# Inverse transform tables by two DMA transposes, smaller first loads, an earlier centroid chain, a last tile stored in halves and a new instruction order

## The chip, the cores and the metric

The kernel runs on one core of a Trainium2 chip. The metric is the device time of one execution in microseconds (us), the median over several runs. The engines are named PE (TensorE, the matrix engine), PEld (its loading of weights, which overlaps matmuls), DVE (VectorE), ACT (ScalarE), POOL (GpSimd) and SP (SyncE, which here only issues transfers). ACT, POOL and SP each have a queue of DMA transfers that they issue.

## The reference, cut to what matters

Clustered attention for 4 batches, 8 heads, 768 rows and 64 columns, then a gated long convolution (a "Hyena" block) over the 768 rows of the 512 joined columns.

```python
# attention: q, k, v [4, 8, 768, 64], centroids [8, 16, 64]
q_n, k_n, c_n = ...                       # each divided by its norm + 1e-6
q_assign = argmax(einsum('bhsd,hcd->bhsc', q_n, c_n), -1)
k_assign = argmax(einsum('bhsd,hcd->bhsc', k_n, c_n), -1)
mask = q_assign[:, :, :, None] == k_assign[:, :, None, :]
attn = softmax(where(mask, q @ k.T / 8, -1e9))
x = (attn @ v) -> [4, 768, 512]
# gate: w_proj [512, 1536], filter_fft [768, 512], w_out [512, 512]
x1, x2, x3 = split(x @ w_proj, 3)
conv = irfft(rfft(x2, 768) * rfft(filter_fft, 768), 768)
out = (x1 * conv * x3) @ w_out            # [4, 768, 512]
```

## The kernel before

**Stages.** The 32 heads of the four batches are taken as eight groups n of four heads, each with two pairs pr of heads, so there are 16 attention passes. A pass goes over six tiles sk of 128 keys. For each key tile PE makes three score products of 128x512 (L689), ACT takes the exponential of each (L698, L701) into one of five buffers p, PE multiplies p with v (L712, four matmuls into one pair of banks), and DVE adds p to a running sum acc (L729 for the first two tiles, L733 after), from which the softmax denominators come (L746 in some passes). The mask is part of the score product: the operands aug hold q or k with extra rows that carry the one-hot cluster of each row (L615 to L658; the one-hot codes are transposed by a DMA, L658).

**Routing.** Before a group's scores, q and k are loaded (load_qk, L299), transposed on PE (L584, L595), multiplied with the normalized centroids in the block table cbd (L504), and the similarities are transposed back (L514) and turned into one-hot codes by DVE (L521 and after). The first group's masks go another way, through first_masks (L494).

**The gate.** After every second group one batch is complete, and hyena (L820) does its gate: forward transform U (L846), products with the spectrum of the filter (L876 into tm, L880 into y), the inverse transform I (L930 to L936), its folding (L942, L952), the gate product y2 (L955), the output product W (L967), a copy to ob (L975) and the store to HBM (L978, L982). Three gates run as filler between attention passes of the next groups; the last has nothing beside it.

**Transform tables.** No FFT is done: the forward table fw and the inverse table inv hold cosines and sines of the 768-point transform, split into even and odd parts. In angles (L345), DVE reduces the angles and ACT takes sines into fw. In tables (L383), six PE operations of 16 transposes in all (L402, L405) turn fw into inv, and eight copies by ACT or DVE (L409, L413) bring the pieces from the banks. tables also loads the filter and makes its spectrum (spectrum, L472).

**Start.** Four loads of 196 KB bring q and k of the first two heads, two each, one head at a time, spread over the idle queues of SP and ACT. centroids (L315) loads the 128x64 centroids on ACT's queue and makes cbd: squares, a sum, a square root on ACT, a Newton step on DVE, a transpose on PE (L336) and two copies on DVE (L339, L340). Those DVE operations stand in one queue with the angle operations of angles.

**Order.** The program records each operation with the engines that may do it, its modelled duration and a due time (Plan.op, L85). place (L114) then lays them out greedily, one engine queue at a time, by due time and modelled readiness. NUDGE shifts the due time of single operations by their number, and ONLY fixes the engine of single operations. So an operation that is added or removed, or a change in a modelled cost, can move any other, and which of ACT, DVE and POOL does an eviction is open except where ONLY fixes it. Each engine does its queue in that order. PE's array works as one 128x128 tile or as two 64-column tiles (product, L70); the placing models a small cost for a change between them.

**End.** With `last` set, the inverse of the last gate sums in the banks (L932), so its fold needs no sd. The last pair of output tiles is stored tile by tile (256 KB each, L978), the others two tiles at once (512 KB, L982).

Of the kernel before, what the change touches and what calls it, by code (L numbers as in the profile page):

```python
# [16 lines left out]
BF16 = mybir.dt.bfloat16  # L17
# [15 lines left out]
NV = 3  # L33
# [3 lines left out]
FIRST = 2  # L37
BUSY = 0.0
# [3 lines left out]
ONLY = {23:"SP",24:"SP",25:"SP",30:"SP",55:"ACT",56:"POOL",59:"ACT",62:"POOL",63:"DVE",75:"ACT",76:"ACT",81:"ACT",83:"DVE",84:"DVE",85:"DVE",87:"ACT",89:"DVE",123:"ACT",125:"DVE",131:"DVE",132:"DVE",134:"DVE",143:"ACT",145:"ACT",149:"ACT",151:"ACT",157:"ACT",161:"ACT",163:"ACT",178:"DVE",179:"DVE",228:"ACT",229:"DVE",235:"POOL",240:"POOL",241:"ACT",246:"POOL",247:"ACT",249:"ACT",250:"DVE",292:"DVE",357:"DVE",358:"POOL",359:"DVE",394:"DVE",404:"ACT",405:"ACT",407:"DVE",409:"DVE",410:"POOL",412:"DVE",416:"ACT",417:"ACT",420:"ACT",462:"POOL",464:"DVE",509:"ACT",514:"ACT",523:"DVE",525:"DVE",526:"DVE",533:"POOL",541:"POOL",549:"DVE",556:"ACT",560:"ACT",563:"DVE",567:"ACT",575:"ACT",578:"POOL",579:"POOL",580:"DVE",582:"ACT",595:"DVE",597:"ACT",601:"ACT",605:"ACT",609:"DVE",610:"DVE",612:"ACT",619:"ACT",624:"ACT",640:"DVE",641:"DVE",690:"ACT",691:"ACT",692:"POOL",693:"ACT",694:"POOL",695:"POOL",697:"DVE",699:"DVE",700:"ACT",701:"ACT",703:"POOL",705:"DVE",747:"DVE",810:"DVE",859:"ACT",860:"ACT",861:"ACT",863:"POOL",864:"ACT",866:"ACT",868:"ACT",871:"DVE",872:"ACT",874:"ACT",916:"POOL",917:"DVE",918:"DVE",965:"DVE",975:"ACT",989:"DVE",990:"POOL",997:"DVE",998:"POOL",1006:"DVE",1008:"ACT",1019:"POOL",1020:"POOL",1021:"DVE",1023:"ACT",1027:"ACT",1035:"DVE",1036:"POOL",1042:"ACT",1046:"ACT",1049:"DVE",1051:"DVE",1053:"DVE",1057:"ACT",1061:"ACT",1064:"DVE",1070:"DVE",1075:"ACT",1078:"ACT",1096:"DVE",1098:"DVE",1146:"ACT",1147:"ACT",1148:"POOL",1150:"ACT",1153:"ACT",1154:"DVE",1156:"ACT",1158:"POOL",1159:"DVE",1162:"ACT",1203:"DVE",1204:"DVE",1205:"DVE",1265:"POOL",1266:"POOL",1314:"ACT",1317:"POOL",1319:"ACT",1322:"ACT",1323:"ACT",1324:"ACT",1326:"POOL",1327:"ACT",1328:"POOL",1330:"ACT",1331:"ACT",1372:"DVE",1373:"DVE",1374:"DVE",1431:"ACT",1435:"DVE",1438:"DVE",1445:"POOL",1446:"POOL",1454:"POOL",1462:"DVE",1464:"ACT",1468:"ACT",1472:"ACT",1475:"POOL",1476:"DVE",1477:"DVE",1483:"ACT",1490:"POOL",1491:"DVE",1492:"DVE",1494:"ACT",1505:"DVE",1506:"DVE",1507:"DVE",1509:"ACT",1517:"ACT",1521:"DVE",1526:"ACT",1529:"ACT",1531:"ACT",1534:"ACT",1536:"ACT",1553:"DVE",1554:"POOL",1601:"ACT",1602:"ACT",1603:"ACT",1604:"ACT",1605:"POOL",1606:"DVE",1607:"ACT",1611:"ACT",1612:"POOL",1613:"ACT",1617:"ACT",1652:"POOL",1713:"DVE",1715:"DVE",1772:"POOL",1809:"ACT",1825:"ACT",1831:"ACT",1837:"DVE",1838:"DVE",1845:"POOL",1853:"POOL",1854:"POOL",1862:"DVE",1869:"ACT",1873:"DVE",1878:"ACT",1886:"ACT",1891:"ACT",1899:"ACT",1904:"ACT",1921:"ACT",1925:"ACT",1932:"ACT"}  # L42
THIRDS = [[(0, 0, 512)], [(0, 512, 768), (1, 0, 256)], [(1, 256, 768)]]
HOLD = {"score": "score", "o": "o"}
AFTER = {"PE": .16}
OVERLAP = {"ACT": .09, "DVE": .08}
MODES = {"pv": 64, "bc": 64, "half": 64, "sim": 32, "den": 32, "score": 0, "proj": 0, "inv": 0}


def array(o, last):  # L50

    return MODES.get(o.kind, 128) or (last if last in (64, 128) else 64)

class Op:
    __slots__ = ("eng", "fn", "due", "deps", "outs", "left", "ready", "end", "start", "on",
                 "alloc", "free", "lat", "lock", "byts", "seq", "kind", "whole", "soft")
# [18 lines left out]
class Plan:  # L78
# [6 lines left out]
    def op(self, eng, fn, due, r=(), w=(), alloc=None, free=(), lock=False, byts=0, after=(), kind=None, lat=0.0):  # L85
# [7 lines left out]
        o.lat = lat  # L93
# [20 lines left out]
    def place(self, free0, banks_for, switch=0.1, wait=0.1, rate=215e3, bonus=0.0, margin=0.02195, shape=0.0):  # L114
        free = dict(free0)
        bank_free = [0.0] * 8
        ready = {e: [] for e in free}
        pend = 0
        st = SimpleNamespace(pool=0.0, dve=0.0, bw={}, last=None, kind=None, score=0, o=0, tail=0,
                             held=dict(score=0, fill=0, o=0))  # L120
# [57 lines left out]
        while any(ready.values()):  # L178
            best = None
            for e, lst in ready.items():  # L180
                f = free[e]
                cand = []
                for o in lst:
                    t = max(f, o.ready)
# [24 lines left out]
            take(o)  # L209
            d = o.eng[e]  # L210
            if e == "PE":
                mode = array(o, st.last)
# [1016 lines left out]
```

## Time and profile before

| | |
|---|---|
| time, median of 3 runs | 382.1 us (381.96 to 382.62) |
| the profiled execution, its span | 380.2 us |
| instructions | 8604 |
| PE, PEld | 363.1 us (96%), 208.0 us (55%) |
| DVE, ACT, POOL | 342.1 us (90%), 267.3 us (70%), 104.8 us (28%) |
| DMA | 47.19 MB, mean 124 GB/s |
| costliest on PE: PV product (L712), scores (L75) | 142.3 us, 73.8 us |
| costliest on DVE: running sums (L733) | 112.5 us, 64 of 1758 ns |
| costliest on ACT: exponentials (L701, L698) | 108.3 us, 57.3 us |

The busy time of an engine is the union of its instructions' times in one profiled execution. The time on the first row is taken without a profile, so the two are close but not the same quantity. Lines of a view of the timeline read: start in us, busy us, engine, line of the code, operation, output, inputs, shapes, number of instructions in the row and, in brackets, the idle time ahead of it and what ended that. Lines of a table by stretches read: from and to in us, length, then busy time and count of PE, PEld, DVE, ACT and POOL, the granted clock of PE as a share of full speed, the mean busy share of the DMA engines, and GB/s. A row on one line of the code reads: least/median/greatest duration in ns, and the first and last start in us.

### The profile page before, as it was taken

How to read it: one execution, taken by the hardware profiler on the slowest of the kernel's cores; microseconds unless marked ns; L12 is line 12 of the kernel's file. 1: busy time of each engine (PE TensorE's matmuls, PEld its weight loads, DVE VectorE, ACT ScalarE, POOL GpSimd, SP SyncE). 2: the span in 40 equal slices, each digit the busy share in tenths (PEclk: the TensorE clock that was granted, in tenths of full speed). 3: DMA queues.
4: the chain of work that ended last, by engine and by line, in shares of the span. 5: the costliest groups of instructions: out<-in, count | busy, mean ns of one | idle time of the engine just before them, and what ended most of it. 6: DMA issues, size and time to landing. Idle time of an engine off the chain costs nothing.

```text
span 380.2 us, 8604 instructions
## 1 busy us (share of the span) xinstructions
PE 363.1 (96%) x3303; PEld 208.0 (55%) x3308; DVE 342.1 (90%) x510; ACT 267.3 (70%) x497; POOL 104.8 (28%) x147
## 2 busy tenths in 40 slices
PE   2799999999999999999999999999999999999995
PEld 2464356445445565655565565565465556566682
DVE  8797997987899999989999999998999998899992
ACT  4896989887886778888757569788864667523332
POOL 8410202122031352231311442333210532202600
PEclk9999999999999999999999999999999999999999
DMA  8527973943869666766776967836646741110314
GB/s 218 124 81 174 207 165 90 189 129 62 208 128 156 117 117 141 125 132 108 167 130 118 239 162 136 166 69 91 104 58 172 123 117 15 46 43 2 127 42 166
DMA packets 93861, 47.19 MB, mean 124 GB/s; under 512 B 82088, under 2 KB 87676, under 8 KB 93820
## 3 DMA queue, kind: packets, MB, share of 16 engines
q1 hardware_dynamic: 88620, 37.03, 40.6%
q0 software_dynamic: 2704, 8.98, 16.7%
q10 hardware_dynamic: 2496, 0.62, 0.7%
q8 instruction: 26, 0.43, 0.5%
q14 instruction: 15, 0.12, 0.1%
HBM read 31.59 MB, written 7.40 MB: 103 GB/s over the span
## 4 chain that ended last, share of the span: by engine, by line
PE 84%; DVE 8%; ACT 4%; issue 1%; DMA 1%; ACTq 0%; POOL 0%; DVEq 0%; POOLq 0%
PE pair L712 32%; PE bank L75 32%; PE bank L584 4%; PE bank L846 4%; PE bank L73 3%; PE bank L615 3%; ACT p L701 2%; PE bank L628 1%; PE bank L595 1%; ACT p L698 1%; PE bank L746 1%; DMA rb<-dr 1%; DVE tm L876 1%; PE bank L504 1%; ACT aug L266 1%
## 5 line engine op out<-in xcount | busy, mean ns | idle before, releaser
L712 PE MATMUL pair<-p,vraw 128*64 128x385 f32 x768 | 142.3, 490 | 0.8 <-ACT osb L736 0.5
L701 ACT ACTIVATE p<-bank 128x512 f32<-128x512 f32 x192 | 108.3, 609 | 26.5 <-PE bank L75 21.8
L733 DVE TENSOR_TENSOR acc<-p,acc 128x1536 f32<-128x1536 f32 x64 | 112.5, 1758 | 6.2 <-ACT p L701 1.6
L712 PEld LDWEIGHTS pair<-p,vraw 128*64 128x64 f32 x768 | 53.6, 136 | 49.0 <-issue 40.9
L75 PE MATMUL bank<-aug,aug 80*64 80x256 bf16 (+3 forms) x680 | 73.8, 327 | 0.6 <-ACT p L701 0.5
L698 ACT ACTIVATE p<-bank 128x512 f32<-128x512 f32 x96 | 57.3, 607 | 7.8 <-PE bank L75 7.4
L75 PEld LDWEIGHTS <-aug 128*64 128x64 bf16 (+1 forms) x680 | 39.3, 109 | 37.5 <-issue 25.2
L766 POOL DMA_DIRECT2D acc<-acc x30 | 23.8, 792 | 111.5 <-DVE acc L733 63.9
L75 PE MATMUL bank<-xT,wpj 128*64 128x384 bf16 x472 | 43.6, 326 | 0.7 <-ACT p L698 0.5
L268 POOL CAST aug<-qkP 64x768 bf16<-64x768 f32 x23 | 20.0, 873 | 79.5 <-ACT qkP L266 30.8
L266 ACT COPY qkP<-bank 128x512 f32<-128x512 f32 (+1 forms) x53 | 27.3, 543 | 15.0 <-PE bank L75 9.0
L75 PEld LDWEIGHTS <-wpj 128*64 128x64 bf16 x472 | 28.7, 110 | 13.7 <-issue 4.5
L75 PEld LDWEIGHTS <-y 128*64 128x64 bf16 x496 | 25.2, 110 | 13.0 <-issue 4.0
L729 DVE TENSOR_TENSOR acc<-p,p 128x512 f32<-128x512 f32 x37 | 25.2, 713 | 5.5 <-ACT p L701 4.8
L876 DVE TENSOR_TENSOR tm<-bank,hm 128x512 f32<-128x512 f32 x44 | 28.0, 682 | 0.5
L880 POOL TENSOR_TENSOR y<-tm 128x512 bf16<-128x512 f32 x17 | 21.5, 1277 | 15.4 <-DVE tm L876 5.4
L266 ACT CAST aug<-qkP 64x768 bf16<-64x768 f32 x29 | 24.0, 830 | 1.3 <-PE bank L75 0.6
L75 PE MATMUL bank<-wout,y 128*64 128x512 bf16 x192 | 23.0, 379 | 0.0
L846 PE MATMUL bank<-wpj,xT 128*64 128x512 bf16 x192 | 22.0, 380 | 0.0
L729 POOL TENSOR_TENSOR acc<-p,p 128x512 f32<-128x512 f32 x11 | 14.2, 1292 | 19.8 <-DVE acc L729 7.8
L584 PEld LDWEIGHTS bank<-ident,qkraw 128*128 128x128 f32 x144 | 15.6, 141 | 5.4 <-issue 3.1
L584 PE MATMUL bank<-ident,qkraw 128*128 128x128 f32 x144 | 18.4, 277 | 0.0
(162 smaller groups left out, 436.1 us busy)
## 6 DMA issues: line engine op xcount, KB each, us to landing
vraw<-in_v_dram SPq DMA_DIRECT2D x16, 384.0 KB, 5.8
qkraw<-in_q_dram SPq DMA_DIRECT2D x31, 192.0 KB, 3.7
qkraw<-in_k_dram SPq DMA_DIRECT2D x30, 192.0 KB, 4.3
rb<-dr SPq DMA_DIRECT2D x30, 192.0 KB, 4.1
out_dram<-ob SPq DMA_DIRECT2D x11, 512.0 KB, 2.9
acc<-acc POOLq DMA_DIRECT2D x10, 384.0 KB, 5.0
acc<-acc POOLq DMA_DIRECT2D x10, 192.0 KB, 4.2
y<-in_moe_filter_fft_dram SPq DMA_DIRECT2D x4, 384.0 KB, 4.2
```

What stands on the lines that cost most here:

```text
L75: T.nc.tensor.matmul(out[64 * i:64 * i + 64], lhsT[:, 64 * i:64 * i + 64], rhs, start=start, stop=stop)
L266: T.nc.scalar.copy(out, in_)
L584: T.nc.tensor.transpose(bank(h.ids[i // 4])[:, ts(i % 4, 128)], raw(ss[i // NT], i % NT), T.ident[:, ::-1] if 3 <= i < NT else T.ident)
L698: T.nc.scalar.activation(o, ap(h).rearrange("p (a b) -> p a b", a=2), Act.Exp, scale=0.125)
L701: T.nc.scalar.activation(flat(s)[:, lo:lo + 512], ap(h), Act.Exp, scale=0.125)
L712: T.nc.tensor.matmul(o[64 * hp:64 * hp + 64, ch, :385], T.vraw[vs][:, hp, sk * D:(sk + 1) * D], T.p[slots[sk]][:, hp, 384 * ch:384 * ch + ...
L729: alu(e).tensor_tensor(o, x, y, op=Alu.add)
L733: T.nc.vector.tensor_tensor(T.acc[os], T.p[slots[sk]][:, :, :S], T.acc[os], op=Alu.add)
L766: op(("POOL", .8), lambda e, rows=rows: T.nc.gpsimd.dma_start(flat_()[:rows], flat_()[rows:2 * rows], accum_op=Alu.add), te, r=[], w=AK, b ...
L846: T.nc.tensor.matmul(ap(h)[64 * i:64 * i + 64], T.xT[xs][:, kt, c:c + 64], T.wpj[:, kt, DM:2 * DM], start=kt == 0, stop=kt == ND - 1)
L876: op(("DVE", .68), lambda e, i=i, cs=cs, r=r, h=h: T.nc.vector.tensor_tensor(T.tm[r][:, cs], ap(h), hmrow(i, (0, 2, 2, 3)[2 * r + cs]), op ...
L880: op({"POOL": 1.5, "DVE": .68}, lambda e, i=i, r=r: alu(e).tensor_tensor(T.y[:, i, r], T.tm[r][:, 0], T.tm[r][:, 1], op=Alu.add if r else ...
```

## The change

1. **Inverse tables.** fw gets a layout of [128, 2, 2, 512] in which the even and odd parts lie 320 columns apart with zeros between (a memset by POOL), so that a plain transpose of a row block gives what inv needs, zeros included. Two `dma_start_transpose` on SP's queue write inv, now [128, 8, 192]. The six PE operations, the eight copies and a memset go. The third part of fw moves into the buffer of w_out, whose load must wait until the filter's spectrum has been made from it. The angle columns are renumbered to fit, which removes two DVE operations and adds an iota on POOL.
2. **First loads.** q and k of the first pair are loaded by three row tiles of one head at a time: eight loads of 98 KB (98,304 bytes) in place of four of 196 KB. The transposes wait only for the piece that they read.
3. **Centroids ahead of angles.** The load of the centroids may go to SP or ACT; the memset of cbd comes earlier on POOL; the placing knows the cost of switching ACT's function tables (`tab`, `TABLE`) and of a slow PE at the start (`COLD`, `SLOW`).
4. **First masks.** A copy with a scale on ACT may make the mask rows that only DVE made before.
5. **Last tile.** The last output tile is copied by halves of 256 columns, one by ACT and one by DVE, and each half is stored by itself, from ACT's and SP's queue.
6. **Order.** Modelled sizes and costs of loads and stores are changed (`RATE`, `LOAD`, `byts`), the banks of the filter's spectrum are of the common class, and NUDGE and ONLY are new throughout. `WHOLE` is 0 and leaves the last gate as it was.

```diff
     def load_qk(n, pr, j, due, after=()):
...
+        src = lambda: (T.q, T.k)[j][n // 2, 4 * (n % 2) + 2 * pr:4 * (n % 2) + 2 * pr + 2].rearrange("h (p t) d -> p t h d", t=NT)
+        for x in range(2):
+            for half in ((0,), (1,)) if n == pr == 0 else ((0, 1),):
+                t = slice(3 * half[0], 3 * half[-1] + 3)
+                op({"SP": .66, "ACT": .66} if n == 0 else ("SP", .66), lambda e, x=x, t=t: dma(e)(
+                    T.qkraw[s][:, t, x], src()[:, t, x]), due, w=[("qkraw", s, x, c) for c in half],
+                   byts=98e3 * len(half), kind="load", after=after, lat=.3 if n else -.5)
...
-        op(("ACT", .4), lambda e: T.nc.scalar.dma_start(cen.c, T.centroids.rearrange("h c d -> (h c) d")), 0,
-           w=["c"], byts=32e3)
+        op({"ACT": .4, "SP": .4}, lambda e: dma(e)(cen.c, T.centroids.rearrange("h c d -> (h c) d")), 0,
+           w=["c"], byts=32e3, kind="load")
...
-        for j in range(6):
...
-                    if j < 4:
-                        T.nc.tensor.transpose(o, T.fw[:k_, j // 2, m, cols:cols + 128], T.identb[:k_, :k_])
-                    else:
-                        for i in range(2):
-                            T.nc.tensor.transpose(o[64 * i:64 * i + 64], T.fw[:k_, i, m, cols:cols + 64], T.identb[:k_, :k_])
...
+        for m in range(2):
+            k_ = 128 - 64 * m
+            op(("SP", 1.3), lambda e, m=m, k_=k_: T.nc.sync.dma_start_transpose(
+                T.inv[:, :, 128 * m:128 * m + k_], T.fw[:k_, m].rearrange("p c x -> p (c x)")), 30.0 + 4 * m, r=FW + ["fw0"],
+               w=[("inv", m)], byts=196e3, lat=3.0)
...
-            hs = [Bank("head"), Bank("head")]
+            hs = [Bank(), Bank()]
...
+                        elif e == "ACT":
+                            T.nc.scalar.activation(o, x, Act.Copy, scale=BIG, bias=-BIG)
...
+                if last and tt == 2 and e_:
+                    for x, (en, q_) in enumerate((("ACT", "ACT"), ("DVE", "SP"))):
+                        cols = ts(x, DM // 2)
+                        op((en, (.35, .42)[x]), lambda e, cols=cols, ob=ob, h=h: copy(e, ob()[:, 1, cols], ap(h)[:, cols]), due + 1,
+                           r=[h], w=[("end", x)], free=[h])
+                        op((q_, .4), lambda e, cols=cols, ob=ob: dma(e)(
+                            T.out[b].rearrange("(p t) m -> p t m", t=NT)[:, NT - 1, cols], ob()[:, 1, cols]), due + 2,
+                           r=[("end", x)], byts=78e3)
...
-        op(("POOL", .6), inv0, 18, w=["inv0"])
+        op(("POOL", .5), lambda e: G().memset(T.fw[:, :, :, 192:320], 0.0), 18, w=["fw0"])
...
-           w=["wout"], byts=1048e3, after=[first[0]], kind="load")
+           w=["wout", ("fw", 2, 0), ("fw", 2, 1)], byts=1048e3, after=[first[0]], kind="load")
```

More of the change, by code (lines that the diff above doesn't have):

```diff
@@ L45 @@
 AFTER = {"PE": .16}
+TABLE = 1.283
+SOON = 0
+RATE = 215e3
+LOAD = 300e3
+COLD, SLOW = 9.5, .95
 OVERLAP = {"ACT": .09, "DVE": .08}
@@ L112, in op, with place @@
         return o
-    def place(self, free0, banks_for, switch=0.1, wait=0.1, rate=215e3, bonus=0.0, margin=0.02195, shape=0.0):
+    def place(self, free0, banks_for, switch=0.1, wait=0.1, rate=RATE, bonus=0.0, margin=0.02195, shape=0.0):
         free = dict(free0)
@@ L118, in place @@
         pend = 0
-        st = SimpleNamespace(pool=0.0, dve=0.0, bw={}, last=None, kind=None, score=0, o=0, tail=0,
+        st = SimpleNamespace(pool=0.0, dve=0.0, bw={}, tab=None, last=None, kind=None, score=0, o=0, tail=0,
                              held=dict(score=0, fill=0, o=0))
@@ L180, in place @@
             for e, lst in ready.items():
-                f = free[e]
                 cand = []
                 for o in lst:
+                    f = free[e] + (TABLE if e == "ACT" and o.tab not in (None, st.tab) else 0.0)
                     t = max(f, o.ready)
@@ L237, in banks_for @@
     if st.o == 0:
-        allowed += [4, 5] if bank.cls == "head" else []
+        allowed += [4, 5] if bank.cls == "head" and st.score <= SOON else []
     elif st.o == st.otiles:
@@ L301, in load_qk @@
         loads.append(1)
-        return [op({"SP": .8, "ACT": .8} if n == 0 else ("SP", .8), lambda e, hp=hp: dma(e)(
-            T.qkraw[s][:, :, hp], (T.q, T.k)[j][n // 2, 4 * (n % 2) + 2 * pr + hp].rearrange(
-                "(p t) d -> p t d", t=NT)), due, w=[("qkraw", s, hp)], byts=196e3, kind="load", after=after, lat=.5)
-            for hp in range(2)]
+        src = lambda: (T.q, T.k)[j][n // 2, 4 * (n % 2) + 2 * pr:4 * (n % 2) + 2 * pr + 2].rearrange("h (p t) d -> p t h d", t=NT)
[5 more added lines that the diff above has]
+                   byts=98e3 * len(half), kind="load", after=after, lat=.3 if n else -.5)
     def load_v(n, pr, due, after=()):
@@ L331, in newton @@
             V().tensor_scalar(cen.cn, cen.c, cen.s1, None, op0=Alu.mult)
[L332 removed]
+        op(("DVE", 1.72), newton, 2.5, r=["s0", "ss", "c"], w=["cn"])
         h = Bank("head")
@@ L584, in tr2 @@
                         T.nc.tensor.transpose(bank(h.ids[i // 4])[:, ts(i % 4, 128)], raw(ss[i // NT], i % NT), T.ident[:, ::-1] if 3 <= i < NT else T.ident)
-                op(("PE", 1.42), tr2, due, r=[("qkraw", s, hp) for s in ss for hp in range(2)] + ["ident"], w=[h], alloc=h)
+                op(("PE", 1.42), tr2, due, r=[("qkraw", s, x, c) for s in ss for x in range(2) for c in range(2)] + ["ident"], w=[h], alloc=h)
                 for c in range(3):
@@ L595, in tr @@
                         T.nc.tensor.transpose(ap(h)[:, ts(t, 128)], raw(s, 3 * ch + t), T.ident[:, ::-1] if ch > j else T.ident)
-                op(("PE", .36), tr, due, r=[("qkraw", s, 0), ("qkraw", s, 1), "ident"], w=[h], alloc=h)
+                op(("PE", .36), tr, due, r=[("qkraw", s, x, c) for x in range(2) for c in ((0, 1) if n else (ch,))] + ["ident"], w=[h], alloc=h)
                 op(EV384 if n != 1 else {"ACT": .48}, lambda e, z=z, ch=ch, h=h: copy(e, T.qkT[z][:, ch], ap(h)[:, :384]),
@@ L815, in attention @@
                free=rk[a_] if last else [], lock=True)
-    INV = [("inv", j) for j in range(4)] + [("inv", j, i) for j in (4, 5) for i in range(2)]
+    INV = [("inv", m) for m in range(2)]
     def hyena(b):
@@ L883, in hyena @@
         if last:
-            op(("ACT", .83), lambda e: T.nc.scalar.activation(T.neg, T.inv[:, 1], Act.Copy, scale=-1.0), A(80),
-               r=INV, w=["neg", ("qkraw", 0, 0), ("qkraw", 0, 1)])
+            op(("ACT", .83), lambda e: T.nc.scalar.activation(T.neg, T.inv[:].rearrange("p (c b) x -> p c b x", c=2)[:, :, 2:], Act.Copy, scale=-1.0), A(80),
+               r=INV, w=["neg"] + [("qkraw", 0, x, c) for x in range(2) for c in range(2)])
         gs, inv = [], []
         for dt in range(ND):
+            whole = last and dt >= WHOLE
             if last:
@@ L922, in hyena, with pair, I @@
             bk = lambda hh, k: bank(hh.ids[k])
-            def I(e, dt=dt, hh=hh):
-                if last:
+            def pair(e_, cs, n, minus, dt=dt):
+                return (T.y[:, 2 if n else e_, cs, ts(dt, 128)],
+                        T.neg[:, cs, 1 - n] if minus else T.inv[:, 4 * cs + (3 - n if e_ else n)])
+            def I(e, dt=dt, hh=hh, pair=pair, whole=whole):
+                if whole:
                     for cs in range(2):
@@ L945, in hyena, with fold @@
             for s_, o_ in ((0, Alu.add), (1, Alu.subtract)):
-                def fold(e, s_=s_, o_=o_, yy=yy, sd=sd, hh=hh, od=od):
+                def fold(e, s_=s_, o_=o_, yy=yy, sd=sd, hh=hh, od=od, whole=whole):
                     o = yy().rearrange("p t (g q) -> p g t q", g=2)
-                    if last:
+                    if whole:
                         x = [y[:, :384].rearrange("p (g t q) -> p g t q", g=2, q=64) for y in (bk(hh, 0), od())]
@@ L952, in fold @@
                     alu(e).tensor_tensor((o[:, ::-1, ::-1, ::-1] if s_ else o)[:, :, :3], x[0], x[1], op=o_)
-                op(("DVE", .55) if last else {"DVE": .55, "POOL": 1.2}, fold, due + 2, r=[hh] + okeys if last else skeys, w=ykeys[s_::2], lock=not last,
-                   free=[hh] if last else [])
+                op(("DVE", .55) if whole else {"DVE": .55, "POOL": 1.2}, fold, due + 2, r=[hh] + okeys if whole else skeys, w=ykeys[s_::2], lock=not whole,
+                   free=[hh] if whole else [])
             op(("DVE", .95) if last else {"DVE": .95, "POOL": 2.1}, lambda e, dt=dt, x3=x3, yy=yy: alu(e).tensor_tensor(
@@ L1008, in constants @@
            r=["kp0"], w=["kp"])
-        def half(e):
-            for i in range(2):
-                h = T.s0t[64 * i:64 * i + 64]
-                T.nc.vector.tensor_scalar(h, h, 0.5 - 383.0 * i, None, op0=Alu.add)
-            T.nc.vector.tensor_scalar(T.s1t, T.s0t, 1.0 / S, None, op0=Alu.mult)
-        op(("DVE", .5), half, .3, r=["s0t0"], w=["s0t", "s1t"])
+        op(("DVE", .2), lambda e: T.nc.vector.tensor_scalar(T.s1t, T.s0t, 1.0 / (2 * S), None, op0=Alu.mult), .3, r=["s0t"],
+           w=["s1t"])
         def small(e):
-            G().memset(T.cbd, 0.0)
-            G().memset(T.half_pi, math.pi / 2)
             for g in range(4):
@@ L1026, in small, with first_ @@
             G().tensor_scalar(T.revx, T.revx, BIG, None, op0=Alu.mult)
-        op(("POOL", .9), small, .4, w=["cbd0", "half_pi", "mk", "revc", "revx"])
+        def first_(e):
+            G().memset(T.half_pi, math.pi / 2)
+            G().memset(T.cbd, 0.0)
+        op(("POOL", .3), first_, .4, w=["cbd0", "half_pi"])
+        op(("POOL", 1.6), small, .4, w=["mk", "revc", "revx"])
         op(("DVE", .3), lambda e: T.nc.vector.tensor_copy(T.identb, T.ident), 3, r=["ident"], w=["identb"])
```

124 lines of the change are left out of this document (55 added, 69 removed).

## The prediction

> **What bounds the kernel now.** I read the page first, then busy time by stretch, then the head and the tail in order of time.
>
> ```profile
> PE 363.1 (96%) x3303; PEld 208.0 (55%) x3308; DVE 342.1 (90%) x510; ACT 267.3 (70%) x497; POOL 104.8 (28%) x147
> ...
> PE 84%; DVE 8%; ACT 4%; issue 1%; DMA 1%; ACTq 0%; POOL 0%; DVEq 0%; POOLq 0%
> ```
>
> TensorE (PE) is busy 363.1 of 380.2 us and carries 84% of the chain that ended last. The 17.1 us without PE work lie at the two ends, as the stretches show (busy us of PE, PEld, DVE, ACT, POOL; clock; DMA share; GB/s):
>
> ```profile
> 0.00:6.00 6.00, 0.00 (x0) 0.00 (x0) 4.35 (x13) 2.14 (x3) 5.28 (x24) 1.00 0.71 162
> 6.00:12.00 6.00, 3.34 (x15) 2.97 (x16) 5.63 (x15) 4.76 (x11) 4.70 (x21) 1.00 1.16 287
> 12.00:23.00 11.00, 10.92 (x85) 6.38 (x84) 8.48 (x19) 9.40 (x19) 2.64 (x9) 1.00 0.46 117
> 23.00:28.00 5.00, 4.85 (x37) 2.84 (x40) 4.41 (x12) 5.00 (x12) 1.65 (x2) 1.00 0.01 3
> ...
> 44.00:318.00 274.00, 271.97 (x2401) 152.39 (x2402) 255.49 (x356) 208.91 (x386) 73.86 (x79) 1.00 0.66 132
> ...
> 372.00:380.00 8.00, 3.50 (x34) 1.65 (x30) 0.69 (x1) 2.73 (x5) 0.00 (x0) 0.91 0.49 197
> ```
>
> From 44 to 318 us PE is busy 271.97 of 274 and DVE 255.49 (93%): PE is the bound, DVE stands close behind. The PE work itself is almost the same in both kernels (below), so the change can gain in the head, in PE's small stalls, and after PE's last matmul. The head in order of time:
>
> ```profile
> 6.07 2.79 PE L595 MATMUL bank<-ident,qkraw 128*128 128x128 f32 x12 [6.07 <-DMA qkraw<-in_q_dram]
> ...
> 9.65 0.16 DVE L326 RECIPROCAL s<-s 128x1 f32<-128x1 f32 x1
> ...
> 11.98 0.21 DVE L339 COPY cbd<-bank 64x64 f32<-64x64 f32 x1
> 12.21 0.22 DVE L340 COPY cbd<-bank 64x64 f32<-64x64 f32 x1
> ...
> 13.09 2.77 PE L504 MATMUL bank<-qkP,cbd 128*32 128x384 f32 x8
> ...
> 15.79 1.29 PE L595 MATMUL bank<-ident,qkraw 128*128 128x128 f32 x6
> ...
> 17.40 0.56 PE L514 MATMUL bank<-ident,sim 64*128 64x64 f32 x6
> ...
> 18.00 0.56 DVE L521 TENSOR_REDUCE mx<-bank 128x24 f32<-128x384 f32 x1 [0.16 <-PE bank L514]
> ```
>
> PE waits for q until 6.07, but the path runs through DVE: the centroid table (cbd) is done at 12.43, behind the angles; then similarities (L504), their transposes (L514, 17.40), the one-hot chain from 18.00, the first score at 22.95 and the first PV product (L712) at 27.36.
>
> **The change, part by part.** The sum is against the profiled span, 380.2 us; the median of the runs shown, 382.1, lies 1.9 above it, and I keep that 1.9.
>
> *Loads in 96-KB pieces.* Q and k of the first head pair come in eight loads, not four. PE's first wait needs two half pieces of k: ahead of them on the queues stand 32 + 4 x 96 = 416 KB at most, where two whole q pieces with the centroids and what ran beside them were 32 + 4 x 192 = 800 KB. At the 287 GB/s of the second stretch that is 1.3 us sooner, so PE starts near 4.8. Four more issues of 0.66 us (the row of the q load on SP) stand on two idle queues. On the path this counts nothing, since the similarities wait for cbd; without that cover it would be worth the 1.3 us.
>
> *Centroids ahead of angles.* In the built order, before cbd DVE has lost the two ops of 1.39 us (L1013) and a small one (0.15), and gained the third fold of the angles (0.52): the ops ahead of cbd sum to 10.99 us before (from 1.34 to 12.43) and 9.97 after. Angles need the wider tables of POOL, whose three iotas and two memsets end near 1.8; 1.8 + 10.1 = 11.9. Six angle ops still stand between the centroid norm and cbd. So L504 can start at 11.9 in place of 13.09; 2.77 + 1.29 later (PE still slow: six transposes in 1.29 us, against 0.88 later), the similarity transposes stand at 15.95. Before, four table transposes (L402, 0.65) came between: 17.40. Gain 1.45.
>
> *From there to the first PV.* The one-hot chain takes 2.8 (18.00 to 20.80) and gives 19.35. Then DVE has a cast, a maximum and two mask rows (0.56 + 0.56 + 0.55 + 0.55): first score near 21.7 (before 22.95). The third mask row comes after two more ops, near 23.1; three exps of 0.6 then give the first PV near 25.0 (before 27.36). Gain 2.35. By then the new order has done three groups of transposes of the next heads less (3 x 0.33) and two scores less (2 x 0.217), and the two table flips (L454) more, each 0.17 plus two changes of the array's tiling at 0.1: 2.35 - 1.42 + 0.74 = 1.7 gained. Bounds: 2.7 if the debt hides under ACT's work, 0.5 if ACT, busy 5.00 of 5.00 us there, must first do the three evictions it still owes (3 x 0.48).
>
> *Inverse tables by DMA.* Sixteen transposes (L402, L405: 0.9 + 0.8 + 0.5 + 0.4 us) and eight evictions (0.25 to 0.32) go; two transposes go onto SP's queue, behind the zeroing of the pads on POOL, near 18. The nearest row:
>
> ```profile
> L658 SPq DMA_TRANSPOSE ohT<-oh x7: 1230/1297/5598, 43.1 to 282.1; - x7
> ```
>
> So they hold SP between 2 x 1.3 and 2 x 5.6 us; I take 2.6, the median, since the 5.6 came with weight loads in flight. Behind them stand the last two k loads of the next heads, the masks of the second pair, v and the filter. PE takes those k near 30.6 (25.0, three PV of 1.3 to 1.45, eleven scores of 0.217); issued at 21, landed 4.3 later (page), they are there. Cost nothing; beyond that it is a rival. The tables themselves are read after 100 us. The Trainium skill, "DMA: Bandwidth & Descriptors", section "Latency and other measured facts", gives DMA transposes 261 GB/s with a strided middle: an estimate of 1.0 us for 256 KB, which would leave SP still less occupied and that rival nearly nothing.
>
> *The new order from 28 to 360 us.* Counted by engine, PE's rows differ by a handful, score tilings are equal, changes of tiling fall from 81 to 74, mostly in the head. PE's start-to-start times there hold some 5.5 us of real waits, so the gain is at most 5.5. ACT loses about 10 us of evictions, DVE gains: five 128x512 evictions into qkP, three into tm, two into ob (0.69 each), five sums of y (0.69). By trace durations, DVE's queue from the first accumulation tile to the fifteenth sums 287 us where it was 274; at the same overlap (255.5/273.6) it would be busy 268 of about 274, 98%. It runs at 98% in single stretches now without PE waiting. I take 0, bounds -3 (half the waits go, as DVE leaves no room for more) and +6.3 (DVE idles 4.3%, near its 4.4% now from 128 to 318).
>
> *The end.* PE's order is the same. The last store is no half: in the built order the 512-KB store of two other tiles still comes last.
>
> ```profile
> 375.54 1.07 ACT L266 COPY ob<-bank 128x512 f32<-128x512 f32 x2 [0.49 <-PE bank L75]
> 376.64 0.33 SPq L982 DMA_DIRECT2D out_dram<-ob  x1
> ```
>
> Now both copies wait for the last matmul (1.07); in the new order one is of an earlier bank: 0.48 less, unless the store that ACT issues between (0.33 to 0.62) eats it. Against that DVE has about 2 us more to do between the last sum of y and the last gate product (two ob copies, one more product), where it idles 1.0 of 12 (360 to 372): up to +0.65. I take -0.15, bounds -0.5 and +0.7.
>
> Sum: -1.7 + 0 + 0 - 0.15 = -1.85: span 378.35, time 380.25, told as 380.3.
>
> **Rivals.** *The order also clears PE's waits:* 3 us more, 377.3. For it: 5.5 us of waits exist, ACT gets lighter. Against: DVE at 98%. *DVE becomes the bound:* from 44 to 318, in order behind evictions it did not have, DVE idles as long as before, accumulations come late, the five p buffers stay full, exps and then scores wait: 268/0.957 = 280 us in place of 274, +6.3, minus 1.85: 386.5; at 3% idle 276.3, 382.6. It decides the sign once DVE idles over 2.8% of that stretch. *The head's gain is given back:* ACT's evictions and the transposes left over refill it before 60 us: 0.5 of head gain less the tail's worst 0.7, or 382.3. *The DMA transposes hold SP:* 11.2 us from 18 gives 29.2; the k loads land near 34, PE stands 3 us at their transposes in order: 383.3; it decides from 8.3 us of holding. And the halved store does not do what it says, as told: already in the sum.
>
> **How the numbers follow.** About 0.2% (0.8 us) is what this measurement tells from no change. Forecast 0.48 (its own range 379 to 381.4, mostly faster); cleared waits 0.22; DVE bound 0.15, of which a third within 0.8 us; given back 0.11 (mostly no change); transposes 0.04. Faster: 0.46 + 0.22 + 0.02 = 0.70; same: 0.02 + 0.05 + 0.07 = 0.14, told as 0.13; slower 0.17. The range reaches from the cleared waits to half the DVE case: 376.9 to 383.8.
>
> **What would show it.** PE's first matmul near 4.8; cbd near 11.9; first score near 21.7; first L708 matmul near 25; the two transposes on SP at 1.3 us each with k in time; DVE's busy share from 44 to 318 near 98% with PE still above 98.5%; the last store of 512 KB issued about 0.8 us after the last matmul's end. Wrong would make it: PE idle rows that name DVE in the middle, a wait for qkraw near 30 us, or a first PV later than 26.

## The result, and the profile after

The changed kernel takes 380.6 us (median of 20 runs, 379.0 to 386.4), the kernel before 382.8 us (median of 20 runs beside them, 381.8 to 386.4): a ratio of 0.9936, 95% interval 0.9914 to 0.9959. The ratio leaves out one slow run of the changed kernel (386.4 us) and so is not exactly that of the two medians. The profiled execution has a span of 378.2 us where it was 380.2.

The first lines of the page and its chain of waits:

```profile
PE 361.6 (96%) x3298; PEld 209.8 (55%) x3298; DVE 348.5 (92%) x516; ACT 257.4 (68%) x483; POOL 106.0 (28%) x148
...
PE 80%; DVE 9%; ACT 3%; SPq 2%; DMA 2%; issue 2%; POOL 1%; ACTq 0%; POOLq 0%; DVEq 0%
```

PE has 1.5 us less to do and is still the bound; DVE has 6.4 us more, ACT 9.9 less. The head in order of time:

```profile
4.16 2.19 PE L591 MATMUL bank<-ident,qkraw 128*128 128x128 f32 x9 [4.16 <-DMA qkraw<-in_k_dram]
...
9.17 0.42 PE L347 MATMUL bank<-ident,sd 128*64 128x128 f32 x1 [2.81 <-DVE sd L344]
...
12.45 2.77 PE L498 MATMUL bank<-qkP,cbd 128*32 128x384 f32 x8 [0.48 <-DVE cbd L353]
...
15.16 1.45 PE L591 MATMUL bank<-ident,qkraw 128*128 128x128 f32 x6
...
18.17 2.68 SPq L407 DMA_TRANSPOSE inv<-fw  x2
...
25.81 1.52 PE L708 MATMUL pair<-p,vraw 128*64 128x385 f32 x8
```

PE starts 1.9 us sooner and then stands still for 2.8 us; cbd is done at 12.31, 0.12 us sooner than before, and the similarities (L498) start 0.64 us sooner. The six transposes at 15.16 still take 1.45 us. The first score follows at 22.55, the first PV product at 25.81: 1.55 us sooner than before.

Then the stretches of 44 to 372 us, first of the kernel before, then of the changed one (length, then busy time of PE, PEld, DVE, ACT, POOL):

```profile
44.00:128.00 84.00, 83.13 (x661) 42.88 (x662) 73.83 (x92) 67.81 (x125) 12.59 (x15) 1.00 0.65 141
128.00:218.00 90.00, 89.78 (x823) 52.73 (x821) 85.86 (x129) 69.63 (x128) 29.37 (x32) 1.00 0.74 141
218.00:318.00 100.00, 99.06 (x921) 56.78 (x919) 95.80 (x139) 71.46 (x135) 31.90 (x33) 1.00 0.60 117
...
318.00:360.00 42.00, 41.58 (x439) 25.64 (x433) 38.50 (x62) 18.69 (x37) 13.57 (x11) 1.00 0.14 46
360.00:372.00 12.00, 11.61 (x192) 9.10 (x192) 10.96 (x19) 3.35 (x7) 0.00 (x0) 1.00 0.12 46
```

```profile
44.00:128.00 84.00, 81.58 (x672) 45.27 (x669) 77.05 (x97) 64.44 (x119) 13.31 (x16) 1.00 0.68 142
128.00:218.00 90.00, 90.00 (x826) 51.50 (x824) 86.94 (x132) 67.89 (x127) 29.99 (x34) 1.00 0.77 145
218.00:318.00 100.00, 99.73 (x935) 58.76 (x933) 95.47 (x139) 70.85 (x133) 31.32 (x30) 1.00 0.60 118
...
318.00:360.00 42.00, 41.86 (x451) 26.56 (x449) 40.75 (x65) 16.74 (x33) 11.92 (x9) 1.00 0.14 46
360.00:372.00 12.00, 12.00 (x177) 8.39 (x173) 10.71 (x19) 3.95 (x8) 0.00 (x0) 1.00 0.12 46
```

PE idles 1.55 us more from 44 to 128 us, and 1.56 us less in the four later stretches (0.22 + 0.67 + 0.28 + 0.39). The table of waits names them. Before (engine, operation waited for: us in total, times, longest):

```profile
PE bank L75 <- ACT p L701: 0.7, 2, 0.5
PE pair L712 <- ACT osb L736: 0.5, 1, 0.5
PE bank L75 <- DVE y L880: 0.5, 1, 0.5
PE bank L75 <- ACT p L698: 0.5, 1, 0.5
PE bank L73 <- ACT p L701: 0.5, 1, 0.5
```

After:

```profile
PE bank L472 <- DVE hm L441: 1.1, 1, 1.1
...
PE bank L472 <- DVE h L441: 0.5, 1, 0.5
PE bank L580 <- ACT tm L437: 0.4, 1, 0.4
...
PE bank L80 <- ACT p L697: 0.2, 1, 0.2
```

Five waits of half a microsecond, spread over the kernel before (ahead of 43.4, 95.4, 219.4, 256.0 and 360.4 us), are gone. In their place stands one cluster of 2.0 us between 56.1 and 62.2 us: the filter's spectrum (L472) has the banks, and neither DVE (L441) nor ACT (L437) empties them in time.

The end is as before but for the last copies:

```profile
373.04 0.38 ACTq L979 DMA_DIRECT2D out_dram<-tm  x1
373.04 0.42 DVE L278 COPY tm<-bank 128x256 f32<-128x256 f32 x1 [1.66 <-ACT tm L276]
373.49 0.33 SPq L979 DMA_DIRECT2D out_dram<-tm  x1
373.51 1.07 ACT L276 COPY ob<-bank 128x512 f32<-128x512 f32 x2 [0.50 <-ACT tm L276]
374.61 0.33 SPq L990 DMA_DIRECT2D out_dram<-ob  x1
```

The halves go out at 373.04 and 373.49, and the 512-KB store of two other tiles still comes last, 0.94 us after PE's last matmul (373.67) where it was 1.14.

By place, the 2.0 us of span are 1.55 ahead of the first PV product, 0.28 from there to PE's last matmul (348.14 us before, 347.87 after) and 0.13 behind it (4.67 and 4.54).

### The profile page after: what moved, and what is told of

Same layout as the page of the kernel before. It is cut to its first block, busy times and chain, and to the rows that moved or that the text cites. A ratio compares the mean times of both kernels' runs of the same rounds, so it can differ in the third digit from the quotient of the medians.

```text
span 378.2 us, 8572 instructions
## 1 busy us (share of the span) xinstructions
PE 361.6 (96%) x3298; PEld 209.8 (55%) x3298; DVE 348.5 (92%) x516; ACT 257.4 (68%) x483; POOL 106.0 (28%) x148
## 4 chain that ended last, share of the span: by engine, by line
PE 80%; DVE 9%; ACT 3%; SPq 2%; DMA 2%; issue 2%; POOL 1%; ACTq 0%; POOLq 0%; DVEq 0%
PE bank L82 32%; PE pair L708 30%; PE bank L842 4%; PE bank L580 4%; PE bank L611 2%; PE bank L80 2%; DMA dd<-den 2%; PE bank L624 2%; SPq L483 1%; SPq L317 1%; DVE tm L872 1%; PE bank L742 1%; ACT p L697 1%; PE bank L591 1%; PE bank L498 1%
## 5 line engine op out<-in xcount | busy, mean ns | idle before, releaser
L708 PEld LDWEIGHTS pair<-p,vraw 128*64 128x64 f32 x768 | 54.9, 136 | 45.2 <-issue 39.0
L82 PE MATMUL bank<-aug,aug 80*64 80x512 bf16 (+3 forms) x680 | 72.7, 327 | 0.2
L82 PEld LDWEIGHTS <-aug 80*64 80x64 bf16 (+1 forms) x680 | 40.7, 109 | 33.8 <-issue 21.7
L276 ACT COPY qkP<-bank 128x512 f32<-128x512 f32 (+1 forms) x47 | 23.5, 543 | 14.3 <-PE bank L580 7.5
L725 DVE TENSOR_TENSOR acc<-p,p 128x512 f32<-128x512 f32 x35 | 23.4, 694 | 2.1 <-ACT p L697 1.6
L725 POOL TENSOR_TENSOR acc<-p,p 128x512 f32<-128x512 f32 x13 | 16.8, 1296 | 22.1 <-ACT p L694 6.9
L276 ACT CAST aug<-qkP 64x768 bf16<-64x768 f32 x25 | 20.7, 829 | 0.7 <-DVE qkP L278 0.2
L732 ACT COPY osb<-pair 128x770 f32<-128x770 f32 x16 | 12.8, 803 | 11.3 <-PE pair L708 11.2
L876 POOL TENSOR_TENSOR y<-tm 128x512 bf16<-128x512 f32 x12 | 15.2, 1273 | 15.6 <-DVE tm L872 6.4
L276 ACT COPY x<-bank 128x384 f32<-128x384 f32 x23 | 11.1, 483 | 12.0 <-PE bank L82 9.6
```

The source lines that it names most:

```text
L82: T.nc.tensor.matmul(out[64 * i:64 * i + 64], lhsT[:, 64 * i:64 * i + 64], rhs, start=start, stop=stop)
L276: T.nc.scalar.copy(out, in_)
L708: T.nc.tensor.matmul(o[64 * hp:64 * hp + 64, ch, :385], T.vraw[vs][:, hp, sk * D:(sk + 1) * D], T.p[slots[sk]][:, hp, 384 * ch:384 * ch + ...
L725: alu(e).tensor_tensor(o, x, y, op=Alu.add)
L876: op({"POOL": 1.5, "DVE": .68}, lambda e, i=i, r=r: alu(e).tensor_tensor(T.y[:, i, r], T.tm[r][:, 0], T.tm[r][:, 1], op=Alu.add if r else ...
```

## The experiments

Parts and order can be told apart, because nearly every operation of one kernel has its counterpart in the other. For each experiment the order of every queue, the engine of every operation and the banks were written down and laid out again, so that an edit moves nothing else:

```diff
-    _, order = build(T)
+    plan, _ = build(T)
+    order = [...]   # operations, engines and banks as written down
```

Below, "old order" is that of the kernel before, "new order" that of the changed kernel; order takes in the choice of engines and banks. All times are medians; each ratio is to the kernel before on the same chip.

### The parts in the old order

Two kernels. The first has the DMA transposes and the new table layout alone; the second has the halved first loads and the halved last tile too. The transposes are put on SP's queue right after the last write of fw.

```diff
-        for j in range(6):              # 16 PE transposes, 8 copies
+        for m in range(2):
+            op(("SP", 1.3), ... T.nc.sync.dma_start_transpose(...)
```

> The kernel before, in its own order on every engine, with the new table layout and the two DMA transposes alone: 16 PE transposes (2.2 us of PE in the trace of before) and eight evictions less, loads and last tile whole. Theory of the prediction (the PE work taken away in the head pays, because PE is the bound, and the DMA transposes hide): 1 to 2.2 us less than before, a ratio of 0.994 to 0.997. Rival (the new order made the gain, the parts nothing): within 0.3 us of before, 0.999 to 1.001. Rival (the transposes hold SP and make the next k late): slower than before by 1 to 3 us, with a wait of PE for qkraw near 30 us.

> All parts of the change but the order: the order of before on every engine, first loads in halves, last tile in halves, DMA transposes. Theory: as the DMA transposes alone, within 0.4 us, since cbd covers the loads and a 512-KB store still comes last. Rival (smaller first loads are worth their 1.3 us): 1.3 us less than that. What then remains to the changed kernel is the order's.

Measured: 383.0 us, ratio 0.9992 (0.9961 to 1.0023), and 383.1 us, ratio 0.9992 (0.9958 to 1.0025). In the traces the first PV product comes 1.0 and 1.3 us sooner than before (26.34 and 26.02), so the work taken off PE is seen in the head. It does not last in these two profiles. With the order fixed, the same matmul of the PV sequence can be compared along the whole run: in the first kernel the lead of 1.0 us becomes a lag of 0.7 us at one place,

```profile
127.28 0.60 PE L81 MATMUL bank<-aug,aug 80*128 80x512 bf16 x3 [1.52 <-DMA aug<-ohT]
```

where PE waits for the mask rows that a DMA brings; in the second the lead falls from 1.3 to 0.6 us by 82 us and to 0.3 us by 298 us. In the second PE starts at 5.90 us, no sooner than in the first with its whole loads (5.58): in the old order the halves do not bring PE's start forward. So the parts without the order made no gain that the times show; a gain of up to 1.6 us is within the intervals. This speaks for the rival, that the order made the gain, and against the theory, though not against the low end of its range (1 us). The new order without the DMA transposes was not run, nor were the earlier centroids by themselves.

### The new order without the halves

```diff
-            for half in ((0,), (1,)) if n == pr == 0 else ((0, 1),):   # 98 KB
+            # whole loads of 196 KB
-                    for x, (en, q_) in enumerate((("ACT", "ACT"), ("DVE", "SP"))):
+                    # the last tile by one copy (ACT) and one store (SP)
```

> The changed kernel in its own order with the first loads and the last tile whole again. Theory of the prediction: the loads are hidden behind the centroid chain and the halves of the last tile end nothing: 0 to 0.4 us more than the changed kernel, ratio to before 0.994 to 0.996; cbd done within 0.2 us of 12.3. Rival: loads worth 1.3 us on the path: 1.3 to 1.7 us more, ratio 0.997 to 0.998.

Measured: 379.8 us, ratio 0.9906 (0.9869 to 0.9943), span 377.2. Neither expectation: it is not slower and looks faster. cbd is done at 12.22, as expected, yet the first PV product comes at 24.76. A kernel with the whole loads alone was run later, on another chip:

> The changed kernel with the first q and k in four whole loads of 196 KB again, the last tile in halves as changed. Theory after the runs before (with halves PE starts at 4.2 us, stands still from 6.4 to 9.2 and keeps its slow clock until after 16 us; with whole loads it starts at 7.8, works without a gap and is fast before 13): first PV near 24.8 in place of 25.8 to 26.0, time 0.5 to 1.2 us less than the changed kernel. Rival (the smaller loads pay): first PV later than in the changed kernel, time 0.5 us more or worse.

Measured: 379.5 us, ratio 0.9904 (0.9868 to 0.994). Its head:

```profile
7.87 2.15 PE L592 MATMUL bank<-ident,qkraw 128*128 128x128 f32 x9 [7.87 <-DMA qkraw<-in_k_dram]
9.81 0.42 PE L348 MATMUL bank<-ident,sd 128*64 128x128 f32 x1
10.03 2.13 PE L592 MATMUL bank<-ident,qkraw 128*128 128x128 f32 x9
...
12.67 2.15 PE L499 MATMUL bank<-qkP,cbd 128*32 128x384 f32 x8
14.76 0.88 PE L592 MATMUL bank<-ident,qkraw 128*128 128x128 f32 x6
...
24.83 1.52 PE L709 MATMUL pair<-p,vraw 128*64 128x385 f32 x8
```

PE starts 3.7 us later than in the changed kernel and then works with hardly a gap. Its similarities take 2.15 us where they took 2.77, and the six transposes 0.88 where they took 1.45. The first PV product comes 1.0 us sooner than in the changed kernel's first profile and 1.2 sooner than in its second (its record is below), and against the second it stays 1.2 to 1.5 us ahead until the last PV product, at 331 us. So the smaller loads cost the head about 1 us here. It is no chance of one profile: with halved loads and nothing added on PE the six profiles of the new order have their first PV product at 25.81 to 26.42, with whole loads three have it at 24.76 to 25.02. In the times it is likely and not shown: the intervals of the ratios overlap that of the changed kernel; three kernels with whole loads and no work added on PE (the third is below) gave 0.9901 to 0.9906, two measurements of the changed kernel 0.9936 and 0.993.

> The changed kernel as it is, on the chip of the next three, as their measure: 380 to 381 us, ratio 0.992 to 0.995. The wait of PE near 56 us for the filter's spectrum (2 us in the first profile) comes again if the order makes it, and is gone if it was chance.

Measured: 380.5 us, ratio 0.993 (0.9904 to 0.9956), span 378.7. The waits at the filter's spectrum are there again to 0.01 us (1.10, 0.48 and 0.40), and the first two in every profile of the new order: the order, with its banks, makes them.

### PE kept busy in the head

```diff
+            for _ in range(13):      # ahead of the centroid transpose
+                T.nc.tensor.transpose(ap(h)[:, :128], T.ident, T.ident)
...
+                for _ in range(4 if pr == 0 and ch else 0):   # ahead of the first similarities
+                    T.nc.tensor.transpose(ap(h)[:, :128], T.ident, T.ident)
```

> The changed kernel with 17 transposes of the identity more, whose results are overwritten: 13 in PE's gap ahead of the centroid transpose and 4 ahead of the first similarity product. Theory (PE runs at half speed in the head until it has been busy for some 3.5 to 5 us without a gap, and the smaller first loads only open gaps): the first similarities take 1.4 to 2.1 us in place of 2.77, and first score and first PV come 1 to 1.7 us earlier than in the changed kernel; the time falls by 0.5 to 1.5 us. Rival (the head's path is DVE's, not PE's clock): similarities as slow as before, first PV within 0.3 us, time the same or up to 1 us more for the added work.

Measured: 380.8 us, ratio 0.9933 (0.9908 to 0.9957). The head does what the theory says: transposes go from 213 to 109 ns each at 10.6 us instead of after 16, the eight similarities take 1.5 us, and the first PV product comes at 24.79, 1.25 us sooner than in the changed kernel beside it. But the time is the same. In the profile the lead is lost at two places (0.9 us near 128 us and 0.7 near 214), the first again at the mask transfer:

```profile
125.81 0.41 PE L84 MATMUL bank<-aug,aug 80*64 80x512 bf16 x2 [1.04 <-DMA aug<-ohT]
```

So PE's clock as a cause of the slow head is shown; that a faster head becomes time, the whole loads make likely and the added transposes do not show. A further kernel put both together with a split last store:

> The changed kernel with whole first loads, the last 512-KB store in two of 256 KB, and transposes of the identity that keep PE busy from 2.6 us on (24 before the first load is there, 6 and 6 in the two gaps after). Theory (the slow clock of the head and the size of the last store each cost what the runs before showed): first similarities at full speed, first PV near 24.2, end 0.4 us sooner: 1.5 to 2.5 us less than the changed kernel, a ratio to before of 0.987 to 0.989. Rival (an earlier head is given back at the mask transfers near 125 us): first PV as early, time within 0.8 us of the changed kernel.

Measured: 381.2 us, ratio 0.9955 (0.9933 to 0.9977). The first PV product is at 24.81, no sooner than with whole loads alone (the similarities start at 13.09: ahead of them a table flip, L454, waits 0.76 us for ACT, and six of the added transposes stand behind it), and PE loses 1.0 us on the whole loads in small steps between 149 and 306 us. Why both kernels with added transposes lose later what they gain is open; none of the runs tells it.

### More and less work on DVE

```diff
-   13 of 26 evictions of 128x512 into qkP on ACT (every second one)
+   the same on DVE, at the same place of the order
```

> The changed kernel with 13 of the 26 evictions of 128x512 into qkP that ACT does moved to DVE, at the same places of the order: DVE does 9 us more, ACT 7.7 less. Theory of the forecast (DVE has room until it is 98% busy, PE stays the bound): within 1 us of the changed kernel. Rival of the prediction (DVE stands so close that more work on it becomes time): 4 to 9 us slower than the changed kernel, PE waiting for exponentials behind full p buffers.

Measured: 386.5 us, ratio 1.0079 (1.0049 to 1.011), 6.0 us above the changed kernel measured beside it.

```profile
44.00:318.00 274.00, 267.94 (x2360) 152.51 (x2358) 260.53 (x372) 194.24 (x362) 73.07 (x78) 1.00 0.67 130
```

9 us more on DVE cost 6. DVE is busy 260.53 of 274 us here, 95%, and PE has lost 3.4 us of this stretch (271.38 in the second profile of the changed kernel). Over this stretch DVE does not come to the 98% that the prediction gave it as room. PE waits above all for qkP (1.3, 1.0 and 0.5 us), and not for exponentials as the rival was told; its price held, its place did not. The other way round:

```diff
-   10 evictions into qkP on DVE
+   the same on ACT, at the same place
```

> The changed kernel with its ten evictions into qkP on DVE moved to ACT: DVE does 6.9 us less, ACT 5.9 more. Theory (from 44 us on DVE is as much the bound as PE, since 9 us more on it cost 6): 1 to 3 us less than the changed kernel. Rival (the order has DVE just below the point where it bounds, PE is the bound there): within 0.5 us, or slower because ACT's exponentials come later.

Measured: 381.5 us, ratio 0.9958 (0.9933 to 0.9984), against 0.993 for the changed kernel: no faster, perhaps 1 us slower, so the rival held. Its profile falls 0.9 us behind at one place, the 96th PV matmul at 70 us, and the lag against the changed kernel shrinks to 0.2 later. That this comes from ACT's added evictions is not shown: the profile of the split store below, in which no engine was changed up to that place, falls 0.9 us behind at the same matmul. What the pair shows is that more work on DVE costs time in the new order and that taking work off it gains nothing that the times show. Whether the cost comes of DVE's load as a whole or of single evictions that wait behind its sums, the run does not separate; the waits for qkP fit both.

### SP held

```diff
-            op(("SP", 1.3), ... T.nc.sync.dma_start_transpose(...)
+            op(("SP", 1.3), ... [T.nc.sync.dma_start_transpose(...) for _ in range(4)]
```

> The changed kernel with each DMA transpose issued four times, eight in all, the same result written again: SP held some 10.7 us in place of 2.7 near 18 us, so the k loads behind it are issued 8 us later, near 29, and land near 33.5. Theory of the prediction: it decides from 8.3 us of holding, so 1 to 3 us slower than the changed kernel, with PE waiting for qkraw after 30 us. Rival (PE takes those k later or has other work): within 0.5 us. If even the 2.7 us cost something, more than 3 us slower.

Measured: 393.2 us, ratio 1.0271 (1.0232 to 1.0311), 12.7 us more. The expectation had the holding wrong. Repeats of one transpose start 2.7 to 3.2 us apart and not 1.3, probably because each writes what the one before wrote and waits for it.

```profile
18.26 20.33 SPq L408 DMA_TRANSPOSE inv<-fw  x8
38.64 1.27 SPq L318 DMA_DIRECT2D qkraw<-in_k_dram  x2
```

```profile
32.11 0.38 PE L83 MATMUL bank<-aug,aug 128*64 128x512 bf16 x2
41.81 2.83 PE L592 MATMUL bank<-ident,qkraw 128*128 128x128 f32 x12 [9.32 <-DMA qkraw<-in_k_dram]
```

The k loads go out 17.65 us later than in the changed kernel (20.99 in its second profile) and PE waits 9.32 us, so 8.3 us of the delay were free. After that wait the twelve transposes take 2.83 us, where such a row takes 1.5 at full speed: the granted clock is 0.50 from 35.0 to 45.2 us. Against the second profile of the changed kernel the first PV product is 0.4 us late, the PV products are 11.3 us late behind the wait, and 12.6 by 200 us; where the last 1.3 came from was not traced. For the change this settles its price: two transposes hold SP 2.7 us, and by this delay (an estimate, 2.7 + 8.3) holding costs nothing up to some 11 us.

### The last store split

```diff
-                T.nc.sync.dma_start(out[tiles 2 and 3], ob())              # 512 KB
+                T.nc.scalar.dma_start(out[tile 2], ob()[:, 0])             # 256 KB, after ACT's copy
+                T.nc.sync.dma_start(out[tile 3], ob()[:, 1])               # 256 KB, after DVE's copy
```

> The changed kernel with the store that does come last (512 KB of two tiles) split into two of 256 KB, the first from ACT's queue, and the last copy on DVE instead of ACT. Theory (what ends last is this store, and a 256-KB store lands in 2.0 us where 512 KB took 2.6 to 3.3): 0.5 to 0.8 us less than the changed kernel, a span near 377.5. Rival (the end is not set by the size of the last store): within 0.2 us of it, or 0.25 us less for the earlier copy alone.

Measured: 380.2 us, ratio 0.9914 (0.9879 to 0.9948). From PE's last matmul to the end of the span are 4.1 us where the changed kernel has 4.54 and 4.53: 0.4 us less, below the expectation, and too little for the times to show. The last copy also went from ACT to DVE here, so the 0.4 is not the split's alone. The whole loads with this split store:

> The changed kernel with whole first loads and the last 512-KB store in two of 256 KB, without any added work on PE. Theory (the head of the whole loads, 1.2 us sooner, is kept to the end as in the run before, and the end is 0.4 us shorter): span near 377.0, time 1 to 1.6 us less than the changed kernel, ratio to before 0.988 to 0.991. Rival (a head that is earlier is given back, as with the added transposes): ratio 0.993 to 0.996.

Measured: 379.6 us, ratio 0.9901 (0.987 to 0.9932), span 377.8. Its first PV product comes at 25.02, and the end takes 4.35 us from the last matmul (4.8 with whole loads alone). The three kernels with whole loads and nothing added on PE (379.5 to 379.8 us) are the fastest that were run, about 1 us below the changed kernel; between them nothing can be told.

## Why the prediction was right, and where it was not

The forecast of 380.3 us met 380.6, and its span of 378.35 met 378.2; as a ratio it was 0.9953 (380.3 to 382.1) and 0.9936 was measured. Of its three terms the sum was right, and partly by luck: the head gave 0.8 us less than forecast, and the new order, forecast at 0, made up for it.

*The head, -1.7.* The direction was right, the path was misread at one step and the size too large. The prediction has the similarities wait for cbd. In the kernel before they did not: cbd was done at 12.43, they start at 13.09 with no idle time of PE ahead of them, behind six transposes in PE's own order.

```profile
11.45 0.42 PE L334 MATMUL bank<-ident,sd 128*64 128x128 f32 x1 [2.59 <-DVE sd L331]
11.67 1.49 PE L595 MATMUL bank<-ident,qkraw 128*128 128x128 f32 x6
```

What PE had waited for was the centroid norm (sd), which came 2.3 us sooner in the changed kernel (9.17). That let PE finish its transposes by 11.5; only then does cbd decide, with a wait of 0.48 us. So cbd came at 12.31, not 11.9, and the similarities gained 0.64 us, not 1.2. The first PV product gained 1.55 and not 2.35. With the debt of transposes and scores that the prediction counted (-1.42 + 0.74), that is 0.9 in place of 1.7, still inside its bounds. PE began at 4.16, sooner than the 4.8 that the smaller loads promised. But that the loads count nothing was wrong, and not for the reason the prediction weighed (a cover that goes): it took PE's slow start as fixed ("PE still slow: six transposes in 1.29 us"), while it depends on how PE is loaded, and the early pieces only moved a gap to 6.4 to 9.2 us. With whole loads the head is about 1 us shorter in this order.

*The DMA transposes, 0.* Right, and the run with SP held confirms the reasoning: the k loads have slack, it decides from about 11 us of holding (8.3 in the prediction, which had PE wanting k at 30.6; it is 32.5), and past that PE stands in order at those transposes. What the prediction did not see is that the 2.2 us of PE work taken away showed no gain in time by themselves: in the old order the lead ran out against a mask transfer or smaller waits.

*The new order, 0.* Two effects hide in it. It clears 2.5 us of PE's waits (five of half a microsecond), near the bound of -3; and it makes a new one of 2.0 us at the filter's spectrum, which the prediction did not look for. The rival of cleared waits was thus half true. As measured the terms are 0.9 in the head, 0.5 here and 0.1 at the end, 1.5 of the 2.0 us of span; what made the rest is open.

Two numbers of this step failed. First, DVE's load: the prediction had 287 us of durations between the first accumulation tile and the fifteenth, where it was 274, and so 268 us of busy time. Measured are 259.46 busy us from 44 to 318 (255.49 before), 4 us more and not 12.5. Summed by time, from 44 to 318 us, DVE's durations are 278.5 us where they were 273.0, and the page has DVE's whole busy time grow by 6.4: more than half of the difference of 13 was work that passed from one side of the two tiles to the other, and not work spread over the stretch. Second, the room: "It runs at 98% in single stretches now without PE waiting" does not hold for the whole; with 9 us more DVE stayed at 95% and the time rose by 6. The rival of DVE as the bound was priced rightly (6.3 us for about 12 us of work on a DVE that cannot go above 95.7%). It did not come true because the order adds only a third of that work there.

*The end, -0.15.* Right: 0.13 us from the last matmul to the end. The last store goes out 0.2 us sooner behind that matmul, by the copy of an earlier bank, and the halves of the last tile end nothing, as the prediction said.

## What to carry to other kernels

Before a count of instructions is read as load on an engine, fix the two ends of the stretch by time and not by a landmark, since work that only crosses the landmark looks like work added. An engine that stands near 95% behind the bound may have no room at all: move known work onto it and see what the time does. And a load that is split to let PE start sooner is a gain only if PE then stays busy; a start followed by a gap can leave it slower than a later start.

## What the runs showed of the hardware

PE's clock in the head depends on gaps. With whole loads PE works from 7.87 us with hardly a gap and is fast by 12.67, at most 4.8 us later; in the changed kernel it works from 4.16 to 6.36 and from 9.17, stands 0.48 us before 12.45, and still takes 213 ns for a transpose at 16.07 (109 to 114 once fast). The traces' own record of the granted clock says the same. Full speed begins in it at 16.4 and 17.0 us in the two profiles of the changed kernel, at 11.9 to 13.0 in the three with whole loads and nothing added, and at 10.7 with 17 transposes added. Ahead of these times it has no entry, so the 1.00 that the tables by stretches give for the head is no reading.

The changes lie on a grid. The stretches at full speed last 361.81, 365.23 or 368.64 us, which is 106, 107 and 108 times 3.413 us, and the half speed that sets in during the 9.3 us wait of the run with SP held lasts 10.24 us, three times that. The Trainium skill, "TensorE: Matmul & The Clock Gate", section "Part 1: The HAM clock gate (the "warmup" mystery)", has half speed until one free-running window of about 3.4 us was busy. The grid agrees with it. How full the window must be the runs do not tell: with all parts in the old order full speed begins at 14.13 us though PE stood 0.56 us in the 3.41 us ahead of it, while in the changed kernel a stretch of that length on the grid with 0.48 us of standing (9.56 to 12.98) did not bring it.

A lead of PE of about 1 us can vanish at one transfer. In the profile with 17 transposes added PE stands 1.04 us for mask rows near 125 us, in that of the transposes alone in the old order 1.52 us near 127. Of the four profiles with whole first loads, whose heads are as early, one has such a wait (0.47 us near 125, with the split store) and three have none. Whether it is chance of the transfer or set by the kernel was not settled.
